# Attention and feed-forward on one core: normalisation in pieces, a gating product moved behind a low part, and running clocks for VectorE's work

## The chip, the cores and the metric

One core of one Trainium2 chip runs the whole kernel. The metric is the device time in microseconds (us) of one execution; the time before is the median of 3 runs.

## What is computed

x has 2048 rows of 512. Two branches are mixed by a gate per row:

```python
g = sigmoid((x * gate_w).sum(-1, keepdims=True))
# A: 32 query heads of 16 on one key/value head
q = (x @ wq) in 32 heads;  k = x @ wk;  v = x @ wv
p = softmax(q @ k.T * 16 ** -0.5);  a = (p @ v, heads joined) @ wo
# B: feed-forward, 512 -> 1792 -> 512
b = silu(x @ w1) @ w2
out = g * a + (1 - g) * b
```

All inputs and the output are float32.

## The kernel before, in words

TensorE's array is used in tiles of 64 rows by 32 columns: eight matmuls of 512 columns run side by side, and such a group of eight is called a **slot** here. Float32 accuracy is had by splitting operands into two 16-bit parts (three products of parts for one).

`attention` (line 726) emits, in an order written out by hand, 32 **rounds** (4 chunks of 512 query rows, 4 groups of 8 heads, 2 halves of a group) of 16 **key steps**. One key step is two score groups: `scores` (L1022) makes one slot of S (L1032), and ScalarE takes its exponential into P (L1035). The product of P with v (`pv`, L1061, matmuls L1078) has two forms. A **split** step uses P's upper 16 bits and a **low part** L that VectorE makes by a subtraction (`low`, L1045 to L1056, two per step): two slots. A **native** step multiplies P in float32: four slots. Only even steps can be split; odd ones are native. `split_step` (L1041) decides: not the first step of a round, and VectorE's backlog below 1.0.

Two key steps make one **cycle** (the loop at L1102). The strings `SPLIT`, `NATIVE` and `PAIR` give its slots: S a score group, F a slot of other matrix work, P one of the two products of a split step, N a native step, B a place for the bound (below). A split cycle is `SFFFSFFFSPPSBN`: 16 slots. **Pair stretches** are three cycles in a row with 8 F each; the second and third end the two F-products of the feed-forward's first layer.

The F slots come from `stream` (L923). It runs the outputs in a fixed order, two at a time: one on the array's upper 64 rows, the next on its lower ones, each into one of two PSUM banks (`pM`). When an output has ended, its eviction is emitted, and the next F slot needs the bank that it frees. Evictions are:

- `ffn_h` (L806): ScalarE's Tanh (L814), then VectorE's **gating product** (L815) in the same breath, then two GpSimd operations (L818, L819) that write H.
- `ffn_o` and `out_proj`: one VectorE accumulation (`add_out`, L736, L745 or L747).
- `q_block` (L840): two VectorE operations (L850, L851), a magnitude (L863) and a DMA.

`bound` (L871) makes a small product for the scores' shift and evicts it on VectorE (L879).

At a round's end `pv` calls `norm_a` (L969): two transposes of the PSUM banks pv (L973, L974), their sum (L975), the digits (L977 to L980), a reciprocal and the quotient into C (L982, L985), all at once. The next round's first product needs the two banks. After a group's second half, `norm_b` (a transpose, L989) and `norm_c` (two operations, L124, L125) follow by `put`, a list of VectorE work with a latest cycle.

`fill` (L782), called at a cycle's end, takes work from that list, then one weight piece (L199, L200) or one operand range check (L139 and L649 to L672), when there is room. Room is reckoned for a cycle at a time: a length of 3.7 or 4.1, less what `spend` (L775) noted, less the backlog that was left.

The emitted order is each engine's order. VectorE, ScalarE, TensorE, GpSimd and the DMA queues wait for each other by semaphores alone.

Of the kernel before, what the change touches and what calls it, by code (L numbers as in the profile page):

```python
# [21 lines left out]
NF = max(GF)  # L22
# [9 lines left out]
        {SPLIT: "SFFFFSFFFFSPPSBN", NATIVE: "SFFFFSFFFFSNBSN"})  # L32

# [16 lines left out]
def kernel(  # L50
# [675 lines left out]
    def attention(ctx, scale_of, t_scale, shifts, split_pieces, chores, q_todo, bounds, early, gates_):  # L726
# [29 lines left out]
        class Out:  # L756


            def __init__(self, terms, evict, hidden=False, is_q=False):
                self.hidden, self.is_q = hidden, is_q  # L760
                self.mm = [(l, r, i, j) for l, r in terms for i, j in ((0, 0), (0, 1), (1, 0))]
                self.evict = evict
# [10 lines left out]
        backlog, spent, todo, cycle = [0.0], [0.0], [], [0]  # L773

        def spend(t):  # L775
            spent[0] += t
# [5 lines left out]
        def fill(length):  # L782
            room = length - backlog[0] - spent[0]
            cycle[0] += 1
            backlog[0], spent[0] = max(0.0, -room), 0.0
            if bounds and turn[0] and turn[1] == 6 and not turn[0].hidden and not turn[0].is_q:
                return
            while todo and (todo[0][0] <= room or cycle[0] >= todo[0][1]):
                t, _, f = todo.pop(0)
                f()  # L790
                room -= t
            if split_pieces.left() and (room >= 1.3 or split_pieces.count < 5.6 + 0.57 * cycle[0]):
                split_pieces.step()
                room -= 1.3
            elif not split_pieces.left() and chores and (room >= 1.1 or cycle[0] > 200):
                if chores[0]:
                    chores[0].pop(0)()
                    room -= 1.1
                elif not open_q:
                    chores.pop(1)()  # L800
                    room -= 1.1
                    if len(chores) == 1:
                        chores.clear()
            backlog[0] = max(0.0, -room)

        def ffn_h(k, f):  # L806
# [4 lines left out]
            def evict(ph):  # L811
# [3 lines left out]
                nc.vector.scalar_tensor_tensor(e, e, 1.0, ph, op0=OP.add, op1=OP.mult)  # L815
# [6 lines left out]
            return Out([(lambda i, b, m, n=32, kt=kt: w1s[b, i, kt, f0 + m:f0 + m + n],  # L822
                         lambda j, b, kt=kt: xs[b, j, kt, cs]) for kt in range(KD)], evict, hidden=1 + f % 2)
# [16 lines left out]
        def q_block(n):  # L840
# [4 lines left out]
            def evict(pq):  # L845
# [5 lines left out]
                nc.vector.scalar_tensor_tensor(q2[:, 1], pq, qsc, q2[:, 0], op0=OP.mult, op1=OP.subtract)  # L851
                nc.sync.dma_start(qd[o, c], q2)
# [7 lines left out]
                spend(1.45)  # L860

            def magnitude(qa):
# [6 lines left out]
                         lambda j, b, kt=kt: xs[b, j, kt, c * 512:c * 512 + 512]) for kt in range(KD)], evict, is_q=True)  # L869

        def bound():  # L871
# [3 lines left out]
            ahead.append(next(seq))  # L875
            ahead[0].bank = pM.tile([128, 512], F32, name="pm")
# [4 lines left out]
            spend(0.6)  # L881
            put(0.6, 3, lambda: (note(), open_q.pop()))
# [26 lines left out]
        def follow():  # L909
# [3 lines left out]
            if o is not None:  # L913
                o.bank = pM.tile([128, 512], F32, name="pm")
            return o

# [6 lines left out]
        def stream():  # L923

            cur = None
            while True:
                if plain[0] and cur is None:
# [7 lines left out]
                    o.evict(o.bank)  # L935
                    yield True
# [7 lines left out]
                if cur and drains[0] == cur.count and ending[0]:  # L944
                    drain()
                for i in range(n):
                    turn[:] = cur, n - i - 1
# [7 lines left out]
                if cur:  # L955
                    cur.evict(cur.bank)
# [225 lines left out]
```

## Time and profile before

| what | value |
|---|---|
| median of 3 runs | 1094.44 us |
| lowest and highest | 1094.07 and 1095.62 us |
| the profiled execution, its time | 1097.11 us |
| its span, first to last instruction | 1095.2 us |
| mean granted TensorE clock | 0.993 |
| instructions in the trace | 63374 |

The profile names engines PE (TensorE matmul), PEld (its weight load), DVE (VectorE), ACT (ScalarE), POOL (GpSimd) and SP (DMA queue). A row of groups has line, engine, operation, output and inputs with their shapes and count, then busy us and mean ns of one, then the idle time ahead of them and what ended it. A row of the timeline has start us, length us and the same names; a number in brackets is the idle time ahead of it and its releaser. The page's table in 40 slices shows PE busy at 9 tenths or more in all slices but the first and the last, ACT from the third to the 39th, DVE between 7 and 9 tenths from the second to the 39th.

### The profile page before, as it was taken

Reading aid. Unit: us, or ns where it says so; the run is one execution under the profiler, and the core shown is the slowest. Engines: PE = TensorE matmul, PEld = TensorE weight load, DVE = VectorE, ACT = ScalarE, POOL = GpSimd, SP = SyncE. Lnnn points to the kernel's source line nnn. Section 1 sums busy time; section 2 is a strip of 40 time slices with the busy share of each in tenths; the row PEclk is TensorE's granted clock in tenths of the full one; section 3 lists DMA queues with packets and bytes.
Section 4 is the critical chain, followed back from the end, with each engine's and each line's share of the span. In section 5 each row is a group of like instructions: output and inputs, shape, how many; then the busy total and the mean of one; then the engine's idle time right before and its main releaser. Section 6 shows DMA issues by size and latency. Waiting matters only on the chain.

```text
span 1095.2 us, 63374 instructions
## 1 busy us (share of the span) xinstructions
PE 1050.2 (96%) x29790; PEld 577.0 (53%) x29790; DVE 899.7 (82%) x1206; ACT 1012.1 (92%) x1121; POOL 215.0 (20%) x170
## 2 busy tenths in 40 slices
PE   8999999999999999999999999999999999999996
PEld 5355556555555445444555555565554555555452
DVE  5779878789988898988879887878789788777975
ACT  5699999999999999999999999999999999999991
POOL 1145205030310220502022004031102014050200
PEclk9899999999999999999999999999999999999999
DMA  5311111210001000000000010000000010000001
GB/s 204 112 49 33 53 53 35 60 50 25 9 21 40 21 21 12 4 21 11 21 12 19 25 39 12 21 12 11 15 13 9 11 50 12 11 12 11 4 4 42
DMA packets 20832, 32.80 MB, mean 30 GB/s; under 512 B 5137, under 2 KB 12050, under 8 KB 20562
## 3 DMA queue, kind: packets, MB, share of 16 engines
q1 hardware_dynamic: 17618, 20.46, 5.9%
q0 software_dynamic: 2512, 8.13, 2.7%
q8 instruction: 235, 3.85, 1.5%
q14 instruction: 35, 0.29, 0.1%
q10 hardware_dynamic: 432, 0.07, 0.0%
HBM read 20.12 MB, written 8.52 MB: 26 GB/s over the span
## 4 chain that ended last, share of the span: by engine, by line
PE 66%; DVE 26%; ACT 5%; issue 2%; DMA 0%; another core or an unknown queue 0%; ACTq 0%; POOL 0%; DVEq 0%
PE pv L1078 23%; PE pm L766 23%; PE S L1032 16%; DVE L L1056 10%; ACT P L1035 4%; DVE T L975 1%; DVE T L973 1%; DVE U L974 1%; DVE e L815 1%; ACT e L814 1%; PE pm L770 1%; DVE O L124 1%; DVE mxs L139 1%; DVE C L985 1%; DVE acc L747 1%
## 5 line engine op out<-in xcount | busy, mean ns | idle before, releaser
L1035 ACT ACTIVATE P<-S 128x1024 f32<-128x1024 f32 x1024 | 968.4, 1067 | 44.0 <-PE S L1032 32.8
L1056 DVE TENSOR_TENSOR L<-P 128x1024 f16<-128x1024 f32 x430 | 531.0, 1281 | 11.1 <-ACT P L1035 11.1
L1032 PE MATMUL S<-qb,KT 50*32 50x512 f16 x8192 | 476.1, 380 | 2.5 <-ACT P L1035 1.4
L1078 PE MATMUL pv<-P,VF 64*32 64x512 f32 x4752 | 333.1, 593 | 0.0
L1032 PEld LDWEIGHTS <-KT 50*32 50x32 f16 x8192 | 189.9, 90 | 229.5 <-issue 158.7
L766 PE MATMUL pm<-w2s,H 64*32 64x512 f16 x5184 | 256.3, 376 | 7.3 <-DVE qx L851 3.1
L766 PE MATMUL pm<-xs,w1s 64*32 64x512 f16 x5376 | 237.7, 376 | 4.1 <-DVE e L815 2.6
L818 POOL CAST H<-e 128x512 f16<-128x512 f32 x56 | 85.2, 1521 | 641.3 <-DVE e L815 639.9
L766 PEld LDWEIGHTS <-w1s 64*32 64x32 f16 x5376 | 119.2, 93 | 64.3 <-issue 20.9
L766 PEld LDWEIGHTS <-H 64*32 64x32 f16 x5184 | 120.4, 93 | 60.4 <-issue 18.8
L1078 PEld LDWEIGHTS pv<-P,VF 64*32 64x32 f32 x4752 | 103.0, 107 | 29.4 <-issue 4.0
L1078 PE MATMUL pv<-L,VP 64*32 64x512 f16 x1720 | 113.6, 375 | 4.5 <-DVE L L1056 3.4
L819 POOL TENSOR_TENSOR H<-e,H 128x512 f16<-128x512 f32 x56 | 106.5, 1902 | 4.5
L1078 PEld LDWEIGHTS <-VP 64*32 64x32 f16 x3440 | 71.0, 93 | 54.0 <-issue 29.4
L1078 PE MATMUL pv<-P,VP 64*32 64x512 bf16 x1720 | 99.4, 388 | 0.0
L766 PE MATMUL pm<-xs,wqs 64*32 64x512 f16 x1152 | 82.8, 375 | 4.2 <-DVE e L815 2.6
L815 DVE SCALAR_TENSOR_TENSOR e<-e,pm 128x512 f32<-128x512 f32 x56 | 38.1, 681 | 40.0 <-ACT e L814 39.8
L973 DVE STREAM_TRANSPOSE T<-pv 128x512 f32<-128x512 f32 x32 | 22.9, 717 | 55.5 <-PE pv L1078 52.9
L766 PE MATMUL pm<-wo_s,O 64*32 64x512 f16 x1440 | 64.3, 375 | 1.1 <-DVE e L815 0.7
L747 DVE SCALAR_TENSOR_TENSOR acc<-pm,g,acc 128x512 f32<-128x512 f32 x48 | 35.8, 746 | 26.5 <-PE pm L766 23.9
L766 PEld LDWEIGHTS <-wqs 64*32 64x32 f16 x1152 | 37.3, 92 | 18.2 <-issue 4.8
L182 POOL DMA_DIRECT2D raw<-in_B_w_dram x27 | 15.3, 568 | 141.8 <-DVE w1s L200 72.3
(168 smaller groups left out, 506.7 us busy)
## 6 DMA issues: line engine op xcount, KB each, us to landing
qb<-qd SPq DMA_DIRECT2D x192, 32.0 KB
raw<-in_B_w_dram POOLq DMA_DIRECT2D x23, 256.0 KB, 3.0
xn<-in_A_x_dram SPq DMA_DIRECT2D x8, 512.0 KB
out_dram<-acc SPq DMA_DIRECT2D x16, 256.0 KB
qd<-qx SPq DMA_DIRECT2D x12, 256.0 KB
raw<-in_A_wo_dram POOLq DMA_DIRECT2D x4, 256.0 KB, 3.0
qb<-sh SPq DMA_DIRECT2D x62, 2.0 KB
raw<-in_B_w_dram SPq DMA_DIRECT2D x3, 256.0 KB
```

The source lines that it names most:

```text
L124: nc.vector.tensor_copy(a1, a)
L182: queue.dma_start(r, src)
L747: nc.vector.scalar_tensor_tensor(a, po, gate[:, n:n + 1], a, op0=OP.mult, op1=OP.add)
L766: nc.tensor.matmul(self.bank[32 * m:32 * m + 32], l(i, rows, 32 * m), r(j, rows), start=first, stop=last)
L815: nc.vector.scalar_tensor_tensor(e, e, 1.0, ph, op0=OP.add, op1=OP.mult)
L818: nc.gpsimd.tensor_copy(H[:, 0], e)
L819: nc.gpsimd.tensor_tensor(H[:, 1], e, H[:, 0], op=OP.subtract)
L973: nc.vector.transpose(T, pv[0])
L1032: nc.tensor.matmul(sc[32 * m:32 * m + 32, f], KT[b:b + 50, k0:k0 + 32], qtile[i][b:b + 50, j], start=True, stop=True)
L1035: nc.scalar.activation(P[:, 2 * j:2 * j + 2], sc, AF.Exp, scale=scale_of(c, o))
L1056: nc.vector.tensor_tensor(lows[s][:, q], P[:, q], upper(P)[:, q], op=OP.subtract)
L1078: nc.tensor.matmul(pvs[i][h][32 * j:32 * j + 32], a[r], b[r, j], start=first, stop=last)
```

## The change

Four things are edited, all inside `attention`; the arithmetic is the same.

- **Normalisation in pieces.** `norm_a` emits only the two transposes. The sum, the digits and the quotient become three entries of the `put` list, due 2, 2 and 3 cycles on. The digits use a small buffer z of their own instead of U. `norm_b` is due 4 cycles on, `norm_c` 2 after it.
- **Gating product.** `ffn_h`'s eviction emits the Tanh and appends the rest to a list `waiting`. `gates_now` empties it behind the next low part that `scores` emits, and at the latest ahead of the next bank or the cycle's end.
- **Running clocks.** `spend`, room and backlog go. `pe`, `act` and `dve` hold estimated times: `on_pe` and `on_dve` advance them per emitted piece of work, with costs written in. Work from the list is emitted when DVE's clock stays within `ROOM` = 2.1 of PE's, or when it is due.
- **Native steps.** `split_step` asks whether DVE's clock is less than `SLACK` = 1.2 past the end of the step's exponentials; a round's first step may be split too.

```diff
+SLACK, ROOM = 1.2, 2.1
...
+        pe, act, dve = [0.0], [0.0], [0.0]
+        def on_dve(t, after=0.0):
+            dve[0] = max(dve[0], after) + t
+            return dve[0]
+        def on_pe(t, after=0.0):
+            pe[0] = max(pe[0], after) + t
...
         def add_out(c, t, po, gate):
             n = c * 4 + t
-            spend(0.68)
...
+            return on_dve(0.74, pe[0])
...
-        def fill(length):
-            room = length - backlog[0] - spent[0]
+        def fits(t):
+            return max(dve[0], pe[0]) + t <= pe[0] + ROOM
+        def fill():
             cycle[0] += 1
...
-            while todo and (todo[0][0] <= room or cycle[0] >= todo[0][1]):
+            while todo and (fits(todo[0][0]) or cycle[0] >= todo[0][1]):
                 t, _, f = todo.pop(0)
+                on_dve(t, pe[0])
                 f()
-                room -= t
-            if split_pieces.left() and (room >= 1.3 or split_pieces.count < 5.6 + 0.57 * cycle[0]):
+            if split_pieces.left() and (fits(1.1) or split_pieces.count < 5.6 + 0.57 * cycle[0]):
+                on_dve(1.1, pe[0])
                 split_pieces.step()
...
                 nc.scalar.activation(e, ph, AF.Tanh, scale=t_scale)
-                nc.vector.scalar_tensor_tensor(e, e, 1.0, ph, op0=OP.add, op1=OP.mult)
-                H = Hs[k, f] = wp.tile([128, 2, 512], F16, name="H", bufs=2 * NF)
-                spend(0.69)
-                nc.gpsimd.tensor_copy(H[:, 0], e)
-                nc.gpsimd.tensor_tensor(H[:, 1], e, H[:, 0], op=OP.subtract)
+                act[0] = max(act[0], pe[0]) + 0.5
+                ready = act[0] + 0.1
+                def gate():
+                    nc.vector.scalar_tensor_tensor(e, e, 1.0, ph, op0=OP.add, op1=OP.mult)
+                    H = Hs[k, f] = wp.tile([128, 2, 512], F16, name="H", bufs=2 * NF)
+                    nc.gpsimd.tensor_copy(H[:, 0], e)
+                    nc.gpsimd.tensor_tensor(H[:, 1], e, H[:, 0], op=OP.subtract)
+                    freed[0] = on_dve(0.68, ready)
+                waiting.append(gate)
+                return 1e9
...
         def follow():
...
             if o is not None:
+                gates_now()
                 o.bank = pM.tile([128, 512], F32, name="pm")
+                o.free = freed[0]
             return o
+        def gates_now():
+            while waiting:
+                waiting.pop(0)()
...
         def norm_a(pv, rb, st):
...
             nc.vector.transpose(T, pv[0])
             nc.vector.transpose(U, pv[1])
-            nc.vector.tensor_tensor(T, T, U, op=OP.add)
-            z = U3[:, :, 0:DIGITS]
...
+            on_dve(1.38, pe[0])
+            def turned():
+                nc.vector.tensor_tensor(T, T, U, op=OP.add)
+            def joined():
+                z = wp.tile([128, 16, 1 + DIGITS], F32, name="z")
...
+            def quotient():
+                r = wp.tile([128, 16, 1], F32, name="rr")
+                nc.vector.reciprocal(r, T3[:, :, 16:17])
...
+            put(0.7, 2, turned)
+            put(1.1, 2, joined)
+            put(0.68, 3, quotient)
...
             if lq and lq[0][0] <= p - 2 and not bound_now():
                 low(*lq.pop(0))
+                gates_now()
         def split_step(s):
-            return steps[s][1] > 0 and backlog[0] < 1.0
+            return dve[0] - ends[2 * s] < SLACK
...
                 norm_a(pvs.pop(i), rb, state)
-                spend(3.1)
                 if rb == 1:
-                    put(0.65, 3, lambda: (norm_b(state), put(1.0, 3, lambda: norm_c(state, (c, o)))))
+                    put(0.7, 4, lambda: (norm_b(state), put(1.1, 2, lambda: norm_c(state, (c, o)))))
...
-            fill(4.1 if pair[0] or ended[0] and ended[0].hidden else 3.7)
+            gates_now()
+            fill()
```

More of the change, by code (lines that the diff above doesn't have):

```diff
@@ L880, in bound @@
             note = q_shift(o, c, s1)
-            spend(0.6)
-            put(0.6, 3, lambda: (note(), open_q.pop()))
+            on_pe(0.06)
+            ahead[0].free = on_dve(0.68, pe[0])
+            put(0.67, 3, lambda: (note(), open_q.pop()))
         urgent = []
@@ L945, in stream @@
                     drain()
+                if new:
+                    pe[0] = max(pe[0], new.free)
                 for i in range(n):
+                    on_pe(0.2165)
                     turn[:] = cur, n - i - 1
@@ L1011, in prefetch @@
                     load_q(qtile[i], c, o, rb, shifts)
-        probs, lows, lq, native = {}, {}, [], set()
+        probs, lows, lq, native, ends, low_end = {}, {}, [], set(), {}, {}
         bounded = [False]
         def bound_now():
-            return bounds and ended[0] and not bounded[0] and not ended[0].hidden and not ended[0].is_q
+            return bounds and ended[0] and not bounded[0] and ended[0].kind == "o"
         def scores(p):
@@ L1075, in pv @@
                     probs.pop(s)
+            on_pe(0.866 if n == 3 else 0.2165, ends[2 * s + 1])
             for j in range(4):
@@ L1115, in attention @@
                 slots = FIRST
-            if not pair[0] and debt[0] >= 6 and s and turn[0] and turn[0].hidden == 1 and turn[1] == 12:
+            if not pair[0] and debt[0] >= 6 and s and turn[0] and turn[0].pair and turn[1] == 12:
                 pair[0] = 3
```

62 lines of the change are left out of this document (33 added, 29 removed).

## The prediction

> **What bounds the kernel now.** I read the page from the top: busy shares, the chain that ended last, the costliest groups.
>
> ```profile
> PE 1050.2 (96%) x29790; PEld 577.0 (53%) x29790; DVE 899.7 (82%) x1206; ACT 1012.1 (92%) x1121; POOL 215.0 (20%) x170
> PE 66%; DVE 26%; ACT 5%; issue 2%; DMA 0%; another core or an unknown queue 0%; ACTq 0%; POOL 0%; DVEq 0%
> L1035 ACT ACTIVATE P<-S 128x1024 f32<-128x1024 f32 x1024 | 968.4, 1067 | 44.0 <-PE S L1032 32.8
> L815 DVE SCALAR_TENSOR_TENSOR e<-e,pm 128x512 f32<-128x512 f32 x56 | 38.1, 681 | 40.0 <-ACT e L814 39.8
> ```
>
> TensorE and ScalarE are both nearly full, yet VectorE, busy 82%, holds 26% of the chain: at places it is late and the other two wait. Shares do not say where, so I cut the loop into its cycles of two key steps (four score groups S each) at the starts of S in the timeline, and asked the busy time of each stretch. The columns are length; PE, PEld, DVE, ACT, POOL busy; granted clock; DMA.
>
> ```profile
> 46.25:1067.01 1020.76, 992.38 (x29293) 547.77 (x29300) 850.63 (x1086) 980.87 (x1072) 208.60 (x142) 1.00 0.09 24
> 421.79:425.46 3.67, 3.67 (x120) 2.00 (x112) 3.02 (x4) 3.67 (x5) 0.00 (x0) 1.00 0.00 0
> 1044.85:1048.74 3.89, 3.89 (x120) 2.08 (x112) 3.46 (x10) 3.89 (x5) 0.00 (x0) 1.00 0.02 4
> 1048.74:1052.34 3.60, 3.27 (x96) 1.58 (x88) 3.60 (x5) 3.54 (x5) 0.00 (x0) 1.00 0.00 0
> 553.79:557.70 3.91, 3.91 (x136) 2.17 (x128) 3.60 (x4) 3.80 (x5) 0.00 (x0) 1.00 0.01 4
> 557.70:561.89 4.19, 4.10 (x137) 2.10 (x128) 2.12 (x4) 4.19 (x6) 1.26 (x1) 1.00 0.00 0
> 561.89:565.93 4.04, 4.04 (x136) 2.10 (x121) 2.29 (x3) 4.04 (x6) 2.48 (x3) 1.00 0.04 10
> 823.71:828.04 4.33, 4.33 (x143) 2.13 (x134) 3.92 (x10) 4.21 (x5) 0.00 (x0) 1.00 0.08 19
> 503.90:510.09 6.19, 4.91 (x137) 2.28 (x128) 5.72 (x12) 5.10 (x6) 0.85 (x1) 1.00 0.03 8
> 404.83:410.73 5.90, 4.29 (x128) 2.17 (x114) 4.92 (x12) 3.85 (x5) 0.00 (x0) 1.00 0.08 20
> 118.83:124.57 5.74, 4.05 (x124) 1.92 (x116) 5.71 (x9) 4.02 (x5) 0.55 (x1) 1.00 0.30 96
> 790.21:798.13 7.92, 6.82 (x122) 2.55 (x127) 5.55 (x11) 4.53 (x5) 1.52 (x2) 0.78 0.11 29
> 46.25:52.94 6.69, 6.69 (x87) 2.89 (x93) 4.74 (x11) 3.51 (x4) 1.57 (x3) 0.51 0.66 186
> ```
>
> The first row is the loop from its second cycle to its last. The next seven are cycles without a stall: split 3.67; native (two exact products) 3.89; split right behind a native one 3.60; the three cycles of a pair stretch 3.91, 4.19, 4.04 (the last two with a Tanh and its gating product); a native one among those 4.33, which over its 20 slots of PE is 0.2165 a slot. The order as built has, in those 254 cycles, 143 split, 28 native, 2 plain ones with a Tanh (4.04), 22, 21 and 25 of the three pair places, and 13 native pair cycles: 524.8 + 108.9 + 8.1 + 86.0 + 88.0 + 101.0 + 56.3 = 973.1 us. The loop took 1020.8, so **47.7 us are lost to stalls**; the last five rows are five of them. The row at 503.90 in detail, DVE first, then ACT and PE:
>
> ```profile
> 504.20 0.72 DVE L973 STREAM_TRANSPOSE T<-pv 128x512 f32<-128x512 f32 x1 [2.85 <-PE pv L1078]
> 505.55 0.69 DVE L975 TENSOR_TENSOR T<-T,U 128x512 f32<-128x512 f32 x1
> 506.27 0.26 DVE L977 TENSOR_TENSOR U<-T,mu 128x96 f32<-128x96 f32 x1
> 507.15 0.25 DVE L982 RECIPROCAL rr<-T 128x16 f32<-128x16 f32 x1
> 507.89 0.71 DVE L989 STREAM_TRANSPOSE T<-C 128x512 f32<-128x512 f32 x1
> 508.53 0.65 DVE L815 SCALAR_TENSOR_TENSOR e<-e,pm 128x512 f32<-128x512 f32 x1
> 505.43 0.62 ACT L814 ACTIVATE e<-pm 128x512 f32<-128x512 f32 x1
> 509.23 0.37 PE L766 MATMUL pm<-xs,wqs 64*32 64x512 f16 x1 [1.28 <-DVE e L815]
> ```
>
> At a round's end (32 of them) the normalisation stands on DVE in one block: two transposes 1.35 us (504.20 to 505.55), their sum 0.72, the digits 0.88, the quotient 0.74, here the transpose back 0.64. The Tanh was done at 506.05; its gating product, which frees PE's bank, began at 508.53, and PE went on at 509.23. Cycles 404.83 and 118.83 are alike, with other evictions behind the block.
>
> **The change, part by part.**
>
> *Split and native.* The built order of the changed kernel has 117 split cycles, 54 native, 2 with a Tanh, 17, 25 and 26 pair ones and 13 native pair ones: 429.4 + 210.1 + 8.1 + 66.5 + 104.8 + 105.0 + 56.3 = 980.1. That is **+7.0 us**; 20 more split cycles stand right behind a native one, at 3.60, which takes back 1.4: **+5.6**. A native step also drops two low parts (378 in the order for 430), here two of them and what follows:
>
> ```profile
> 427.12 2.36 DVE L1056 TENSOR_TENSOR L<-P 128x1024 f16<-128x1024 f32 x2 [0.31 <-ACT P L1035]
> 429.40 1.21 DVE L139 TENSOR_REDUCE mxs<-w2s 128x1 f32<-128x1024 f16 x1
> 424.46 2.35 DVE L1056 TENSOR_TENSOR L<-P 128x1024 f16<-128x1024 f32 x2
> 423.75 0.42 PE L1078 MATMUL pv<-P,VP 64*32 64x512 bf16 x8
> ```
>
> One holds DVE 1.14 us (427.12 to 429.40), so 59 us of DVE work go, but off the path: they show only where DVE is late, which the stalls below count.
>
> *Normalisation in pieces.* Work is the same; only the transposes stay at the round's end. In the order, sum and digits still leave together 22 times, so the largest block behind the transposes is 1.6 us instead of 2.3 to 3.0.
>
> *Gating product behind the next low part* (55 of 56). A typical pair cycle shows the room:
>
> ```profile
> 557.42 1.93 ACT L1035 ACTIVATE P<-S 128x1024 f32<-128x1024 f32 x2
> 559.88 0.69 DVE L815 SCALAR_TENSOR_TENSOR e<-e,pm 128x512 f32<-128x512 f32 x1 [2.07 <-ACT e L814]
> 560.48 1.22 DVE L1056 TENSOR_TENSOR L<-P 128x1024 f16<-128x1024 f32 x1
> 561.02 0.41 PE L766 MATMUL pm<-xs,w1s 64*32 64x512 f16 x8
> ```
>
> DVE waits 2.07 us for the Tanh while the low part could run: its exponential was done at 559.35. In the new order: low part from 559.4 to 560.5, product to 561.2, where PE wants the bank at 561.02. So it is 0.2 late in the middle pair cycle, and in the last one, where two exponentials stand ahead of the Tanh, not at all. Behind the product on DVE stand the second low part, used a cycle later, and the pieces; GpSimd's casts start later by at most 1.1 us, and it is busy 20%. No queue but DVE's is passed.
>
> *What stays lost.* (a) In 12 middle pair cycles transposes or pieces stand right ahead of low part and product. For the row at 503.90: transposes from 0.30 after the cycle's start, 1.35, sum 0.72, low part 1.14, product 0.65: 4.16, where PE wants the bank at 3.32 (561.02 - 557.70). 0.84 late; where only transposes or one piece lead, about 0.3, behind two pieces up to 1.2. I take 0.7: 8.4 us. Such lateness shows nearly whole: 6.19 was 1.86 over the native 4.33, with the product 1.96 late. (b) The other 15 middle ones, 0.2 each: 3.0. (c) Round ends now carry low parts ahead of the transposes. With an accumulation in the cycle, the low parts from 424.46 end 1.27 after the next cycle begins, the transposes at 2.62, while the next round's first product wants its bank at 1.96 (423.75 - 421.79). 0.66 late in 9 rounds, of which ScalarE's pace covers about half: 2.7. (d) Scattered small ones elsewhere: 2.0, an estimate between nothing and 20 times the 0.29 by which 4.19 exceeds its 18 slots.
>
> *Start.* Step 0 is now split, so two low parts (2.27) stand ahead of the bound's eviction:
>
> ```profile
> 44.86 0.39 PE L367 MATMUL pm<-qx,kab 64*32 64x512 f16 x2 [2.06 <-DVE O L851]
> 45.66 0.68 DVE L879 TENSOR_SCALAR qx<-pm 64x512 f16<-64x512 f32 x1
> ```
>
> That eviction ends at 48.6 instead of 46.3, and PE's next product waits for it. The cycle at 46.25 runs at a granted clock of 0.51 and takes 6.69, 2.8 over a native one. The new one has 15 slots to go at 48.6: 10 at half clock until 52.9, 5 at full clock, end at 54.0, 1.0 later than now; if the half clock lasts through it, 2.2 later. I take 1.0: start 3.8. The Trainium skill, "TensorE: Matmul & The Clock Gate", section "HAM oscillation — how this bites in real kernels", says that PE should have no idle gap above about 3.4 us. The trace differs: a gap of 2.06 us stands right before the half clock; by the page a longer start wait would cost no clock, and the start would stay at 1.0.
>
> *Range check* (a DMA to DRAM and back).
>
> ```profile
> SPq L658 <- DMA md<-raw: 7.9, 1, 7.9
> ```
>
> In the cycle at 790.21 this write was still to land; it is 4.0 over a native one, by a stall and a clock of 0.78. I keep it. The check now follows the gather by two cycles instead of three, so DVE may wait up to 2 us for the row: +1.0, bounds 0 and 2.2 (below nothing if the pause falls elsewhere: -4.0).
>
> *Sum.* Lost after: 3.8 + 5.0 + 8.4 + 3.0 + 2.7 + 2.0 = 24.9 against 47.7, so -22.8; cycles +5.6: **-17.2 us**. Renamed buffer z, planner constants and the tail behind the loop cost nothing: same instructions, and the last normalisation is one chain as now. Span 1095.2 becomes 1078.0; the profiled execution, 1097.1, 1079.9; it stood 2.7 over the median of 1094.44, so **1077 us**.
>
> **Rivals.**
> 1. *ScalarE covers the rest.* (a) to (d) vanish because PE, with 3.46 us of slots in a 3.67 cycle, catches up: 16 us less, 1061. For: short waits are made good in the split cycles. Against: 6.19 showed no cover.
> 2. *DVE is still late at round ends.* Two low parts and the transposes meet where the old order had a free DVE (2.85 us idle ahead of 504.20, the round's first step being native). If (a) to (d) cost 27 instead of 16: 1088. If they cost 33, nothing is gained.
> 3. *Slower: the product becomes PE's wait.* Behind a whole low part (1.14, less the 0.46 between 560.56 and 561.02) in both pair cycles, 54 times 0.68 is 36.7, where (a) and (b) hold 11.4: 1102. It decides from 0.53 us a product on. For: PE's banks are two and it waits for one at 509.23. Against: DVE's 2.07 idle ahead of the product.
> 4. *The pieces are none.* In the order sum and digits leave together 22 times, and the sum leaves with the transposes 10 times. If such blocks hold up what PE waits for as the whole one does, 17 of the 24.8 us taken as recovered at round ends (40.9 now, 16.1 after) stay lost and pay for the native cycles: 1094, no change. Against: the block in front of a product shrinks from 3.0 or more to 1.6.
>
> **How the numbers follow.** Forecast, 1077 give or take 7: 0.52. Rival 1: 0.15. Rival 2: 0.18. Rival 4: 0.05. Rival 3: 0.10. The range from 1061 to 1092 takes in rivals 1 and 2 and leaves out 3 and most of 4. About 0.2%, 2 us, is what a measurement of this kernel can tell from no change: faster 0.85, same 0.05, slower 0.10.
>
> **What would show it.** Right: the cycles after a round's end fall from 6.2 to about 5, no DVE block over 1.6 us between transposes and product; DVE's idle time ahead of the product (39.8) falls by half or more; low parts x378; native cycles still 3.89. Wrong: PE waiting for e in ordinary middle pair cycles by 0.5 or more (rival 3), PE waiting for U at the first product of most rounds (rival 2), or half clock in more windows than now. What would upset the sum is a price per native cycle other than 0.22.

## The result and the profile after

The changed kernel took 1085.29 us (median of 4 runs, 1085.09 to 1085.50) beside 1095.03 for the kernel before: ratio 0.991, 95% interval 0.9892 to 0.9927. The profiled execution took 1085.09 (1097.11 before): 12.0 less where 17.2 were forecast. The 1085.29 stands between the forecast (1077 give or take 7) and rival 2's 1088.

The page of the changed kernel, the lines that answer to those shown of before (busy shares, the chain that ended last, three of the costliest groups):

```profile
PE 1047.3 (97%) x29790; PEld 577.1 (53%) x29790; DVE 846.5 (78%) x1154; ACT 1012.0 (93%) x1121; POOL 178.2 (16%) x170
PE 69%; DVE 19%; ACT 9%; issue 2%; POOL 0%; DMA 0%; ACTq 0%; SPq 0%; POOLq 0%; DVEq 0%
L1080 ACT ACTIVATE P<-S 128x1024 f32<-128x1024 f32 x1024 | 968.3, 1062 | 31.0 <-PE S L1077 20.0
L1104 DVE TENSOR_TENSOR L<-P 128x1024 f16<-128x1024 f32 x378 | 470.5, 1274 | 101.7 <-ACT P L1080 101.3
L829 DVE SCALAR_TENSOR_TENSOR e<-e,pm 128x512 f32<-128x512 f32 x56 | 38.1, 680 | 1.6 <-ACT e L824 0.6
```

DVE's share of the chain fell from 26% to 19%. The exponential waited 31.0 us, 13.0 less than before: about the whole gain. DVE's 40.0 idle us ahead of the gating product are 1.6 now; it waits 101.7 ahead of low parts instead (11.1 before). By itself that is free time on DVE and not yet a shorter program; e5 below tries it alone. Low parts are 378, as forecast.

Windows of the changed kernel: the loop, a split and a native cycle, and the cycles that answer to the stalled ones of before (length; PE, PEld, DVE, ACT, POOL busy; clock; DMA):

```profile
46.32:1054.94 1008.62, 989.38 (x29305) 547.58 (x29312) 798.26 (x1035) 980.89 (x1072) 171.82 (x142) 1.00 0.09 24
807.51:811.18 3.67, 3.67 (x121) 1.99 (x112) 3.36 (x4) 3.67 (x5) 0.00 (x0) 1.00 0.02 4
121.02:124.91 3.89, 3.89 (x120) 2.19 (x112) 3.82 (x8) 3.84 (x5) 0.00 (x0) 1.00 0.20 72
403.13:406.83 3.70, 3.70 (x122) 2.00 (x114) 2.66 (x5) 3.64 (x5) 0.00 (x0) 1.00 0.08 23
498.45:503.44 4.99, 4.46 (x137) 2.06 (x129) 4.66 (x6) 4.69 (x6) 0.85 (x1) 1.00 0.02 4
783.17:788.90 5.73, 3.88 (x115) 1.98 (x119) 5.70 (x9) 4.15 (x5) 2.70 (x2) 1.00 0.04 10
46.32:54.29 7.97, 5.87 (x87) 2.89 (x93) 6.71 (x12) 3.58 (x4) 1.67 (x3) 0.57 0.51 155
244.08:249.02 4.94, 3.86 (x120) 2.14 (x112) 4.94 (x7) 3.87 (x5) 0.00 (x0) 1.00 0.04 11
382.13:387.69 5.56, 4.28 (x136) 2.00 (x128) 5.49 (x7) 4.89 (x6) 0.84 (x1) 1.00 0.01 3
```

The loop is 1008.62 for 1020.76, so the whole change lies in it. Split and native cycles still cost 3.67 and 3.89. Two cycles behind a round's end that took 5.90 and 5.74 (404.83, 118.83) now take 3.70 and 3.89, the one of 6.19 takes 4.99. At the prediction's prices the order costs 980.1 us and **28.5 are lost** (47.7 before; 47.6 in the table below, where only the total is rounded): 4.3 in the second cycle of all, 14.1 in middle pair cycles, 3.0 at the range check (the cycle at 783.17 and the one ahead of it), 7.1 elsewhere. The last two rows are kinds of stall that need a reason: a round's end at 244.08 and a middle pair cycle at 382.13.

The first of them on DVE in the changed kernel, and the two products of PE that waited (a number in brackets is the idle time ahead):

```profile
243.41 0.74 DVE L757 SCALAR_TENSOR_TENSOR acc<-pm,g,acc 128x512 f32<-128x512 f32 x1
244.07 2.35 DVE L1104 TENSOR_TENSOR L<-P 128x1024 f16<-128x1024 f32 x2
246.33 0.71 DVE L1006 STREAM_TRANSPOSE T<-pv 128x512 f32<-128x512 f32 x1
246.97 0.67 DVE L1007 STREAM_TRANSPOSE U<-pv 128x512 f32<-128x512 f32 x1
...
247.09 0.38 PE L1129 MATMUL pv<-P,VP 64*32 64x512 bf16 x1 [0.86 <-DVE T L1006]
247.69 0.42 PE L1129 MATMUL pv<-P,VP 64*32 64x512 bf16 x7 [0.21 <-DVE U L1007]
```

Two low parts of the new round's first step, now split, stand ahead of the transposes. PE wants the bank that they empty and waits 0.86 and then 0.21. How often this happens, beside the largest of PE's waits in the loop (us in all, times, the longest):

```profile
PE pm L779 <- DVE e L829: 9.9, 13, 1.6
PE pv L1129 <- DVE U L1007: 1.5, 7, 0.2
PE pv L1129 <- DVE T L1006: 0.9, 1, 0.9
```

So the picture at 244.08 is the only one of its size; with the smaller ones the transposes hold PE for 2.4 us in all, and the gating product for 9.9.

### The profile page after: what moved, and what is told of

The parts are those of the page before. It is cut to its first block, busy times and chain, and to the rows that moved or that the text cites. A ratio compares the mean times of both kernels' runs of the same rounds, so it can differ in the third digit from the quotient of the medians.

```text
span 1083.2 us, 63321 instructions
## 1 busy us (share of the span) xinstructions
PE 1047.3 (97%) x29790; PEld 577.1 (53%) x29790; DVE 846.5 (78%) x1154; ACT 1012.0 (93%) x1121; POOL 178.2 (16%) x170
## 4 chain that ended last, share of the span: by engine, by line
PE 69%; DVE 19%; ACT 9%; issue 2%; POOL 0%; DMA 0%; ACTq 0%; SPq 0%; POOLq 0%; DVEq 0%
PE pm L779 25%; PE pv L1129 24%; PE S L1077 17%; DVE L L1104 9%; ACT P L1080 8%; DVE e L829 2%; DVE T L1006 1%; DVE U L1007 1%; PE pt L318 1%; PE pm L783 1%; ACT e L824 1%; DVE T L1011 1%; DVE z L1015 0%; DVE acc L757 0%; PE pk L132 0%
## 5 line engine op out<-in xcount | busy, mean ns | idle before, releaser
L1104 DVE TENSOR_TENSOR L<-P 128x1024 f16<-128x1024 f32 x378 | 470.5, 1274 | 101.7 <-ACT P L1080 101.3
L1077 PE MATMUL S<-qb,KT 50*32 50x512 f16 x8192 | 457.0, 380 | 3.6 <-ACT P L1080 1.2
L1129 PE MATMUL pv<-P,VF 64*32 64x512 f32 x5168 | 352.5, 590 | 0.0
L779 PE MATMUL pm<-w2s,H 64*32 64x512 f16 x5184 | 251.6, 375 | 4.7 <-DVE e L829 4.2
L779 PEld LDWEIGHTS <-w1s 64*32 64x32 f16 x5376 | 112.2, 93 | 70.9 <-issue 27.1
L1129 PE MATMUL pv<-P,VP 64*32 64x512 bf16 x1512 | 90.7, 390 | 2.3 <-DVE U L1007 1.5
L1129 PE MATMUL pv<-L,VP 64*32 64x512 f16 x1512 | 86.3, 375 | 0.1
L832 POOL TENSOR_TENSOR H<-e,H 128x512 f16<-128x512 f32 x56 | 71.5, 1276 | 4.5
L1129 PEld LDWEIGHTS <-VP 64*32 64x32 f16 x3024 | 56.1, 94 | 29.2 <-issue 9.8
L757 DVE SCALAR_TENSOR_TENSOR acc<-pm,g,acc 128x512 f32<-128x512 f32 x48 | 35.8, 745 | 40.8 <-PE pm L779 38.6
L779 PEld LDWEIGHTS <-O 64*32 64x32 f16 x1440 | 31.0, 93 | 15.7 <-issue 3.9
L184 POOL DMA_DIRECT2D raw<-in_B_w_dram x27 | 14.8, 550 | 120.9 <-DVE w1s L202 69.9
```

The costliest lines, as they stand in the source:

```text
L184: queue.dma_start(r, src)
L757: nc.vector.scalar_tensor_tensor(a, po, gate[:, n:n + 1], a, op0=OP.mult, op1=OP.add)
L779: nc.tensor.matmul(self.bank[32 * m:32 * m + 32], l(i, rows, 32 * m), r(j, rows), start=first, stop=last)
L1077: nc.tensor.matmul(sc[32 * m:32 * m + 32, f], KT[b:b + 50, k0:k0 + 32], qtile[i][b:b + 50, j], start=True, stop=True)
L1104: nc.vector.tensor_tensor(lows[s][:, q], P[:, q], upper(P)[:, q], op=OP.subtract)
L1129: nc.tensor.matmul(pvs[i][h][32 * j:32 * j + 32], a[r], b[r, j], start=first, stop=last)
```

## The experiments

All ratios are those of medians, to the kernel before on the same chip. The runs were on several chips, on which the kernel before had medians of 1093.42 to 1095.31. For each trace the cycles were also cut at the starts of S and priced as in the prediction. "Lost" is the loop less the price; "ends" are the first three cycles of the rounds without middle pair ones.

| kernel | median us | ratio, 95% interval | native | price | lost | of it 2nd cycle | middle pair | ends |
|---|---|---|---|---|---|---|---|---|
| before | 1095.03 | 1 | 41 | 973.1 | 47.6 | 2.8 | 13.8 | 19.8 |
| changed | 1085.29 | 0.991 (0.9892-0.9927) | 67 | 980.1 | 28.5 | 4.3 | 14.1 | 6.8 |
| e1 pieces only | 1069.54 | 0.9772 (0.9755-0.9788) | 45 | 974.3 | 18.3 | -0.2 | 3.1 | 4.6 |
| e2 product at once | 1089.54 | 0.9949 (0.9934-0.9965) | 67 | 980.1 | 31.0 | 3.3 | 5.9 | 14.6 |
| e3 whole block | 1120.28 | 1.0254 (1.0228-1.0279) | 67 | 980.1 | 62.6 | 3.0 | 26.6 | 29.4 |
| e4 slack 2.4 | 1083.50 | 0.9896 (0.9878-0.9914) | 22 | 968.8 | 38.6 | 4.3 | 12.7 | 11.2 |
| e5 pieces, queued | 1071.45 | 0.9782 (0.9769-0.9795) | 45 | 974.3 | 20.5 | 2.6 | 7.5 | 3.8 |
| e6 mixed | 1085.92 | 0.9916 (0.9903-0.993) | 67 | 980.1 | 28.6 | 3.8 | 2.4 | 10.5 |
| e7 step 0 native | 1081.20 | 0.9881 (0.9864-0.9899) | 68 | 980.2 | 23.3 | -0.2 | 14.2 | 5.9 |
| e8 e1, no rule | 1081.82 | 0.9879 (0.9862-0.9896) | 35 | 971.8 | 32.1 | 0.1 | 6.1 | 13.9 |
| e9 rule back | 1080.86 | 0.9887 (0.9861-0.9912) | 87 | 985.1 | 17.6 | -0.2 | 14.8 | 0.2 |
| e10 rule, slack 2.4 | 1069.54 | 0.9774 (0.9748-0.9799) | 41 | 973.3 | 19.3 | -0.2 | 10.6 | 0.7 |
| e11 e1, rule alone | 1081.71 | 0.9881 (0.9856-0.9906) | 32 | 971.6 | 32.0 | 0.1 | 6.0 | 4.7 |
| e12 e10, no piece | 1073.78 | 0.9804 (0.9784-0.9824) | 46 | 974.8 | 21.8 | 2.7 | 4.6 | 1.9 |

Theory 1 at the outset: the pieces are the gain; product behind a low part, native cycles and start give some of it back. Its rivals put the gain into the moved product (A) or the clocks (B).

**e1, the pieces alone** in the kernel before:

```diff
-            nc.vector.tensor_tensor(T, T, U, op=OP.add)
...
+            put(0.7, 2, turned)
+            put(1.1, 2, joined)
+            put(0.68, 3, quotient)
...
-                spend(3.1)
+                spend(1.38)
...
-                    put(0.65, 3, lambda: (norm_b(state), put(1.0, 3, lambda: norm_c(state, (c, o)))))
+                    put(0.7, 4, lambda: (norm_b(state), put(1.1, 2, lambda: norm_c(state, (c, o)))))
```

> The kernel before, with one part of the change: behind a round's two transposes the sum, the digits and the quotient leave as three pieces in later cycles. The old planner (a length of 3.7 or 4.1 less what was charged), the old rule for native steps and the product at once behind the Tanh stay; the order has 422 low parts (430 before, 378 after) and 45 native cycles (41, 67). Theory 1 (the gain is the normalisation broken up; the late product and the native cycles give some of it back): at least the whole change's gain, because the product stays early and there are only 4 native cycles more (0.9 us): 1078 to 1086. Rival A (the gain comes from the product moved off DVE's 39.8 us of waiting): 1091 to 1096, as before. Rival B (it comes from the running clocks, which place native steps where DVE is late): 1089 to 1095.

1069.54: 25 faster than before and 16 faster than the whole change, 8 beyond theory 1's range. The pieces are more than the whole gain; A and B fall as sources of it. What gives 16 us back?

Two things stand in the way of reading the 25 as the smaller block alone. In 20 of the 31 rounds that end in the loop the list had room at once, so sum and digits still left right behind the transposes and only the quotient went to a later cycle. And from the loop's cycle 66 on (counted from 0) the pair stretches stand in other cycles than before: the output projections enter the F slots after `norm_c`, which here leaves at cycle 68 and in the kernel before at cycle 66. Five middle pair cycles (81, 97, 113, 129 and 241) then no longer follow a round's end, where they lost 9.4 us together. The changed kernel, e2, e3, e6, e7 and e9 have the old places but for one stretch; e4, e5, e10, e11 and e12 have those of e1, e10 up to cycle 195. e3 and e8 tell the pieces and the places apart.

**e2, the product at once** in the changed kernel, the order else kept:

```diff
                 def gate():
-                    nc.vector.scalar_tensor_tensor(e, e, 1.0, ph, op0=OP.add, op1=OP.mult)
-                    H = Hs[k, f] = wp.tile([128, 2, 512], F16, name="H", bufs=2 * NF)
-                    nc.gpsimd.tensor_copy(H[:, 0], e)
-                    nc.gpsimd.tensor_tensor(H[:, 1], e, H[:, 0], op=OP.subtract)
                     freed[0] = on_dve(0.68, ready)
```

The four lines stand ahead of `def gate` here.

> The changed kernel, but the gating product and GpSimd's two operations stand right behind the Tanh as before, the clocks being kept as they were so that all else in the order is the same (378 low parts, 67 native cycles). Theory 1 (behind the low part the product frees the bank late in the middle pair cycles, 13.7 us in all over the 4.19 of one without a stall): most of that comes back, 1074 to 1080. Rival A (the gain comes from the moved product): 1090 to 1096. Rival C (the low part that now waits behind the product, and the Tanh, is as late for its second product as the product was for the bank): 1083 to 1087, as after.

1089.54, missed by all three: 4 slower than the changed kernel. The middle pair cycles did gain (14.1 to 5.9), but the round ends lost as much (6.8 to 14.6): PE's waits for the transposes rose from 2.4 us to 7.8. Only 2.5 of the 5.1 us between the two profiled executions lie in the loop; 1.8 lie ahead of it, where e2's clock is at 0.50 from 45.5 us on, and 0.9 behind it.

**e3, the whole block** in the changed kernel:

```diff
-            put(0.7, 2, turned)
-            put(1.1, 2, joined)
-            put(0.68, 3, quotient)
+            turned()
+            joined()
+            quotient()
+            put(0.7, 2, lambda: None)
+            put(1.1, 2, lambda: None)
+            put(0.68, 3, lambda: None)
```

> The changed kernel, but sum, digits and quotient leave in one block behind the two transposes, as in the kernel before; three empty pieces hold their places in the planner so that all else in the order is the same (378 low parts, 67 native cycles). Theory 1 (the pieces are the whole gain, and what else changed costs): slower than the kernel before, 1096 to 1108, since the block now stands with low parts and the late product. Rival A or B (product or clocks are the gain, and the pieces matter little): 1085 to 1089. The prediction's fourth rival (the pieces are none): 1084 to 1087.

1120.28, slower still than theory 1 said. The rest of the order is the same here, the places of the pair stretches too, so in the changed order the pieces alone are worth 35 us (34 of them in the loop). In the old one it was 25: whatever else the change does makes DVE later where the block stands.

**e4, slack 2.4**:

```diff
-SLACK, ROOM = 1.2, 2.1
+SLACK, ROOM = 2.4, 2.1
```

> The changed kernel with one number changed: a step is split as long as the running clock of DVE stands less than 2.4 us, not 1.2, behind the step's exponential. The order has 468 low parts (378 after) and 22 native cycles (67), so DVE gets 103 us more work. Theory 1 (many native steps relieve a DVE that isn't late): 45 native cycles fewer at up to 0.22 are 10 us, of which some goes in new waits: 1076 to 1084. Rival B (native steps where DVE is late are the gain): DVE is late at the rounds' ends again, 1089 to 1100.

1083.50, within theory 1's range, yet hardly a gain: 45 native cycles fewer save 11.3 of price and lose 10.1 in new waits. So native cycles do relieve something, only not all of them at a profit.

**e5, e1 with the product queued** behind the next low part:

```diff
+                def gate():
                     nc.vector.scalar_tensor_tensor(e, e, 1.0, ph, op0=OP.add, op1=OP.mult)
...
+                waiting.append(gate)
...
                 low(*lq.pop(0))
+                gates_now()
```

> The kernel of e1 (1069.5; pieces, old planner, 422 low parts, 45 native cycles) with the gating product and GpSimd's two operations queued behind the next low part, as in the change; every other instruction stays in its place, so that this is the queueing alone. Theory 1 (the queued product frees the bank late in the middle pair cycles, which lost 14.0 in the changed kernel and 3.1 in e1): 8 to 12 slower than e1, 1077 to 1082, with middle pair cycles of 4.33 to 4.5 where e1 has about 4.3. Rival D (the queueing is free, and the 16 us between e1 and the changed kernel belong to the clocks, which choose other cycles for pieces and native steps): 1068 to 1072.

1071.45: rival D. The intervals of e1 and e5 overlap. The middle pair cycles lose 4.4 more and the split ones 4.6 less; 2.8 of the rest are a half clock in the second cycle that e1 doesn't have. **Theory 1's late product falls.**

**e6, the product at once in the middle pair cycle only**, the changed kernel else:

```diff
+                now = pair[0] == 2
+                if now:
+                    product()
...
                 def gate():
+                    if not now:
+                        product()
                     freed[0] = on_dve(0.68, ready)
```

`product` holds the four lines of the product.

> The changed kernel, but the product stands right behind its Tanh in the middle pair cycle alone and behind the low part elsewhere; clocks and order otherwise as in the changed kernel. e2, with all products early, lost only 6.0 in the middle pair cycles but 10 more in split, native and first pair cycles. Theory 1: the last cycle of a stretch, where the queued product cost nothing (0.9 over 26 cycles), keeps its free place, so the middle ones gain without the rest losing all of it: 1077 to 1083. Rival C (the clocks have put pieces where DVE is free only if it doesn't wait for the Tanh, so the early product makes the cycles behind it late whichever it is): 1084 to 1090.

1085.92: rival C. The middle pair cycles lost 2.4 for 14.1, and other cycles 11.8 more. The wait went elsewhere: 9.7 of these 11.8 lie two cycles behind a middle pair one, 0.3 in the cycle right behind it. The work on DVE is the same in sum, but why it shows there no run separates.

**e7, step 0 native** in the changed kernel:

```diff
-            return dve[0] - ends[2 * s] < SLACK
+            return s > 0 and dve[0] - ends[2 * s] < SLACK
```

> The changed kernel with step 0 native again (376 low parts, 68 native cycles), so that no low parts stand ahead of the bound's first eviction. Theory 1 (the start's second cycle, 7.97 now and 3.73 in e1, is long by a wait behind those low parts and by a half clock that follows): 1.3 to 4.3 faster than the changed kernel, 1081 to 1084. Rival (only the phase of the clock's fall matters, since e1 has the same gap of 2.06 ahead of it and no half clock): 1085 or, if the fall happens to stay away, 1082.

1081.20, 4.1 less and at theory 1's end. The profiled execution has neither the wait nor the half clock, so this run doesn't tell the two apart. Elsewhere a half clock without that wait cost 2.6 to 2.8 in the second cycle (before, e5, e12), which would leave some 1.5 of the changed kernel's 4.3 to the wait, an estimate.

**e8, e1 without the rule that a round's first step is native**:

```diff
-            return steps[s][1] > 0 and backlog[0] < 1.0
+            return s > 0 and backlog[0] < 1.0
```

> The kernel of e1 without the rule that a round's first step is native (except step 0), so native steps come only from the old planner's backlog: 442 low parts, 35 native cycles for 45; by class prices 972.1 for 974.6. Theory 1 (in pieces, a round's end needs no relief by a native step): 1066 to 1069. Rival E (the native first step is what leaves DVE free for the transposes, and two low parts ahead of them make PE wait at the next round's first product): 0.5 to 1 in most of 31 rounds, 1074 to 1090.

1081.82: rival E, 12 slower for 10 native cycles less; 30 of the rounds' 32 first steps turned split and 20 others native. This rule went with the change, beside the clocks. The same cycle of step 306 in e8 (one of 5.05 us) and, second, in e1 (3.90):

```profile
653.26 2.76 DVE L1066 TENSOR_TENSOR L<-P 128x1024 f16<-128x1024 f32 x2
655.95 0.70 DVE L973 STREAM_TRANSPOSE T<-pv 128x512 f32<-128x512 f32 x1
656.58 0.67 DVE L974 STREAM_TRANSPOSE U<-pv 128x512 f32<-128x512 f32 x1
...
656.70 0.38 PE L1088 MATMUL pv<-P,VP 64*32 64x512 bf16 x1 [0.88 <-DVE T L973]
657.30 0.42 PE L1088 MATMUL pv<-P,VP 64*32 64x512 bf16 x7 [0.21 <-DVE U L974]
```

```profile
644.87 0.72 DVE L973 STREAM_TRANSPOSE T<-pv 128x512 f32<-128x512 f32 x1 [1.69 <-PE pv L1088]
645.51 0.67 DVE L974 STREAM_TRANSPOSE U<-pv 128x512 f32<-128x512 f32 x1
646.22 0.69 DVE L977 TENSOR_TENSOR T<-T,U 128x512 f32<-128x512 f32 x1
```

In e8 the two low parts hold the transposes to 2.4 us after the cycle's start (653.58), in e1 nothing does: they follow PE's last product at once, 0.3 us after the cycle's start (644.57). It is the picture of the changed kernel at 244.08, and more often: in e8 PE waits 7.4 us for the transposes, in e1 not at all.

e8 also settles what e1 left open. Up to cycle 129 its pair stretches stand where those of the kernel before do, and the middle cycles 81, 97 and 113, which lost 1.86 each behind a round's end, lose nothing. Cycle 97 before, then in e8:

```profile
436.72:442.91 6.19, 4.91 (x139) 2.28 (x130) 5.74 (x12) 5.08 (x6) 0.87 (x1) 1.00 0.03 8
```

```profile
430.31:434.50 4.19, 4.19 (x136) 2.40 (x128) 3.43 (x6) 4.19 (x6) 1.26 (x1) 1.00 0.04 11
```

So the pieces do it without new places. In cycles 2 to 65, where the places are those of before in all kernels, e1 lost 3.6 less than the kernel before and e8 3.3 more than e1.

**Theory 2**: the loss of 14 against e5 belongs to the new native rule, which takes native steps away from the rounds' first ones (3 of 32 are left) and puts them where they relieve less. Rival F: the clocks place the pieces badly, whatever the rule.

**e9, the rule back** in the changed kernel; **e10, the same with slack 2.4**:

```diff
-            return dve[0] - ends[2 * s] < SLACK
+            return steps[s][1] > 0 and dve[0] - ends[2 * s] < SLACK
```

> The changed kernel with the old rule added to its new one: a round's first step is native always, other steps by the running clocks as before. 338 low parts, 87 native cycles (67 in the changed kernel, of which 3 stand first in a round); by class prices 985.4 for 980.4. Theory 2 (theory 1's late product fell with e5; the 16 us lost against e1 belong to the new native rule, which leaves a round's first step split, as taking the rule from e1 cost 12 in e8): the stalls fall by 12 or more, the class prices rise by 5, so 1073 to 1080. Rival F (the clocks put pieces into the wrong cycles, whatever the rule): 1084 to 1092.

> The kernel of e9 with the slack of the clocks at 2.4 us instead of 1.2: 430 low parts, 41 native cycles, 32 of them a round's first; by class prices 973.5. Theory 2: the natives that count are kept and those that relieve nothing are gone, so about e5's 1071.5 with 1.1 less in class prices: 1066 to 1072. Rival F: like e4 (1083.5), which has the same slack without the rule: 1080 to 1085. If all natives beside the first ones were relief, it would be slower than e9.

1080.86, a touch over the range in which theory 2 had it and below F's, and 1069.54, right in it. The stall at 244.08 is gone, here in e10, the cycle and its DVE rows:

```profile
236.88:240.78 3.90, 3.90 (x121) 2.14 (x113) 3.65 (x6) 3.90 (x5) 0.00 (x0) 1.00 0.05 11
```

```profile
236.23 0.74 DVE L757 SCALAR_TENSOR_TENSOR acc<-pm,g,acc 128x512 f32<-128x512 f32 x1
237.18 0.72 DVE L1006 STREAM_TRANSPOSE T<-pv 128x512 f32<-128x512 f32 x1 [0.21 <-PE pv L1129]
237.82 0.67 DVE L1007 STREAM_TRANSPOSE U<-pv 128x512 f32<-128x512 f32 x1
```

The cycle is 0.23 dearer by price and 1.04 shorter. The four kernels make a table of two by two: without the rule 1085.29 and 1083.50 (slack 1.2, 2.4), with it 1080.86 and 1069.54. At slack 2.4 the rule adds 19 native cycles (4.5 us by price) and takes 19.3 of losses; at slack 1.2 it adds 20 (5.0) and takes 10.9; 4.5 of either are the second cycle. Given the rule, the 46 native cycles that slack 1.2 adds over 2.4 cost 11.8 and take 1.7: they relieve next to nothing. The slack also moves the list's pieces and, from cycle 66 on, the pair stretches, so this is the slack's whole effect. In cycles 2 to 65, with the places alike, nine more native cycles cost 2.1 and the losses rise by 0.4, so the reading doesn't hang on the places.

**e11, e1 with the rule alone** and no native step by backlog:

```diff
-            return steps[s][1] > 0 and backlog[0] < 1.0
+            return steps[s][1] > 0 and backlog[0] < 90.0
```

> The kernel of e1 with native steps at the rounds' first steps alone (the backlog may grow without limit): 448 low parts, 32 native cycles for 45; by class prices 971.8 for 974.6. Theory 2 (only a native step at a round's end is worth its 0.22): 2 to 3 faster than e1, 1066 to 1068. Rival G (the other 13 stand where DVE is late and spare a wait each): 1070 to 1078.

1081.71: nearest rival G, though 3.7 beyond its range, so theory 2 was too strong. The rule isn't enough: 13 native cycles by backlog, 2.7 us of price, spare 13.7, together with the list, whose order follows the same backlog. 9.8 of these lie ahead of the loop's cycle 60, where weights are still split on DVE (16.6 lost there, 6.8 in e1).

Theory 2 is also too strong on where the 14 us go. Of the 13.8 us by which the changed kernel's loop is longer than e5's, 5.8 are the price of 22 more native cycles, 6.6 lie in the middle pair cycles, 3.0 at the round ends and 1.7 in the second cycle; the rest is 3.3 shorter. PE waits 9.9 us for the gating product in the changed kernel and 2.7 in e5, which queues it too. With clocks and queue the middle pair cycles lose 10.6 to 14.8 (changed, e4, e9, e10), with the old planner and the queue 7.5. So what the clocks put ahead of the product has a part in it, and no run separates that part from the places of the stretches.

**e12, e10 with nothing of the planner's list ahead of a middle pair cycle**:

```diff
+            if pair[0] == 3:
+                return
             while todo and (fits(todo[0][0]) or cycle[0] >= todo[0][1]):
```

> The kernel of e10 (1069.5) in which nothing of the planner's list (pieces of the normalisation, splits, range check) leaves at the end of the first cycle of a pair stretch, so that on DVE low part and gating product of the middle cycle have nothing of it ahead; 420 low parts, 46 native cycles, by class prices 975.0 for 973.5. In e10 a piece left there in 23 of 27 stretches, and the middle cycles lost 10.6. Theory 3 (what the middle cycles still lose is the work ahead of the low part, and the queued product itself costs at most 0.23 there): 4 to 5 off the middle cycles, 1.5 on for the native ones: 1065 to 1068. Rival H (work kept from one cycle is late in the next, as in e6): 1069 to 1074.

1073.78: rival H. The middle pair cycles fell from 10.6 to 4.6 (0.17 each), more than theory 3 said. Against these 6.0 stand 1.5 of price, 2.9 of a half clock in the second cycle, and 5.6 in the other cycles. As in e6, much of the wait moved: up to cycle 204, where the stretches of e10 and e12 stand alike, the middle cycles lose 4.0 less, and those two and four cycles behind them 3.4 more. No run beat e1 and e10, 2.3% faster than before and 1.4% faster than the change.

## Why the prediction was right, and where it was not

The sign and the stated range (1061 to 1092) held, the size did not: 1085.29 lies above the forecast's own 1070 to 1084. At the profiled execution 1079.9 was forecast and 1085.09 came, 5.2 more. The forecast had also taken 2.7 off for the median; the changed kernel's profiled execution stands at its median.

- *Split and native.* The prices held (3.67, 3.89, and 3.60 behind a native cycle). What the prediction left out is what a native cycle spares at its place: it priced 26 more of them at +5.6, left the relief to the stalls, and put no figure on the 29 rounds that lose theirs in the first step. Where they stand decides. Without the second cycle, 31 more first-step cycles and 13 fewer others take 14.8 us of stalls for 4.3 of price at slack 2.4 (e4, e10); 28 more and 9 fewer take 6.4 for 4.8 at slack 1.2 (changed, e9); 30 fewer and 20 more, in e8, bring 13.5 and save 2.5. That is about 0.5, 0.2 and 0.5 us a first step, an estimate that gives the others nothing, and they cost 0.22 to 0.25. One of the others that slack 1.2 adds takes 0.04 for 0.26 (1.7 and 11.8 over 46).
- *Round ends.* Rival 2 named the mechanism, two low parts and the transposes meeting; its 1088 was 3 too high. Of that wait itself, (c), the prediction had the size nearly right: 2.7 in 9 rounds, and PE waits 2.4 in 8. So it isn't what made the forecast too low; it is part of what the old rule would have saved.
- *Normalisation in pieces.* Right. The prediction had 24.8 us recovered outside the start and the range check (40.9 to 16.1); 19.7 came (40.9 to 21.2). Alone in the old order the pieces, with the places that move with them, are worth 25.3 (from 1094.84, the kernel before in e1's comparison). Rival 4 falls by e3, where the whole block costs 35. That sum and digits left together 24 times in e1 cost little there. Rival 1 falls too: the losses (a) to (d) that it lets vanish came to 21.2.
- *Gating product.* DVE's wait went, as said. As a price the queueing is nothing, by e5; in the changed kernel PE waits 9.9 us for the product, but e6 and e12 took much of such a wait away without a gain. Rival 3 falls.
- *(a) and (b)* gave the sizes nearly right: 11.4 forecast, 14.1 measured. By what DVE had ahead of the low part: two steps of the list, or the transposes and one, in 11 cycles, 8.4 us; one or none in 16 cycles, 5.6, where 3.0 was forecast. The cycle at 498.45 lost 0.80 over 4.19 where 0.84 was worked out:

```profile
498.75 0.72 DVE L1006 STREAM_TRANSPOSE T<-pv 128x512 f32<-128x512 f32 x1 [0.60 <-PE pv L1129]
499.39 0.68 DVE L1007 STREAM_TRANSPOSE U<-pv 128x512 f32<-128x512 f32 x1
500.10 0.69 DVE L1011 TENSOR_TENSOR T<-T,U 128x512 f32<-128x512 f32 x1
500.71 1.22 DVE L1104 TENSOR_TENSOR L<-P 128x1024 f16<-128x1024 f32 x1
501.84 0.68 DVE L829 SCALAR_TENSOR_TENSOR e<-e,pm 128x512 f32<-128x512 f32 x1
```

One of the three dearest, at 382.13, had more ahead than any row of before suggested, on DVE, then PE and GpSimd:

```profile
380.03 3.20 DVE L1104 TENSOR_TENSOR L<-P 128x1024 f16<-128x1024 f32 x2
383.16 0.70 DVE L1033 STREAM_TRANSPOSE T<-C 128x512 f32<-128x512 f32 x1
383.89 0.43 DVE L126 CAST O<-T 128x512 f16<-128x512 f32 x1
384.36 0.69 DVE L127 TENSOR_TENSOR O<-T,O 128x512 f16<-128x512 f32 x1
384.96 1.22 DVE L1104 TENSOR_TENSOR L<-P 128x1024 f16<-128x1024 f32 x1
386.10 0.68 DVE L829 SCALAR_TENSOR_TENSOR e<-e,pm 128x512 f32<-128x512 f32 x1
...
386.83 0.37 PE L779 MATMUL pm<-xs,wqs 64*32 64x512 f16 x1 [1.19 <-DVE e L829]
...
379.79 1.22 POOL L832 TENSOR_TENSOR H<-e,H 128x512 f16<-128x512 f32 x1
```

Two low parts took 3.20 for 2.35, the first beside GpSimd's subtract (the last section has more on that), and the transpose back and the two operations of the cast, which the prediction didn't list, left together, 1.9 us: PE waited 1.19.

- *(c) and (d)*: 7.1 measured where 4.7 was forecast, less the 1.4 that it credited to cheap cycles: +3.8, the largest term that was mis-sized. With (c) at 2.4, most of it is (d).
- *Start*: 3.8 forecast over a native cycle; 4.1 measured (7.97 less 3.89). *Range check*: 5.0 forecast, 3.0 measured. The check did come too early, as the prediction said: DVE waited 3.57 us for the row (2 at most was forecast) and PE 1.63 for the product behind it; what fell away is the half clock of before.

```profile
782.02 0.39 DVE L666 TENSOR_REDUCE raw<-raw 1x32 f32<-1x128 f32 x1 [3.57 <-DMA raw<-md]
...
785.22 0.84 PE L779 MATMUL pm<-w2s,H 64*32 64x512 f16 x24 [1.63 <-DVE e L829]
```

Together: +0.5 at the start (counted over its own price, 4.3), -2.0, +2.7 in the middle pair cycles, +3.8 elsewhere: 5.0 of the 5.2.

Open: whether another slack or backlog gives less than e1 and e10, and what the range check would cost if it were read later; no run tried them.

## What to carry to other kernels

Price a relief by what stands behind it at its place: here a native step first in a round bought some 0.2 to 0.5 us for about 0.24, and others almost nothing or 1 us (e10, e11). When an order is rewritten, look for the rule that went out with the old planner, and change one part at a time: one part of this change was worth 2.3%, the others took 1.4 of that back. See too what else an edit moves: e1 also moved the pair stretches, and only e3 and e8 told the two apart. A wait that was removed by reordering an engine's queue, without taking work off it, stood a few cycles further on here (e6, e12).

## What the runs showed of the hardware

The same wait of PE ahead of the loop is followed by a half clock in some executions and not in others. The changed kernel, then e7: PE's gap, and the next cycle's window (the granted clock is the number ahead of the DMA share):

```profile
45.03 0.39 PE L369 MATMUL pm<-qx,kab 64*32 64x512 f16 x2 [2.06 <-DVE O L868]
48.82 0.62 PE L779 MATMUL pm<-xs,w1s 64*32 64x512 f16 x4 [2.10 <-DVE qx L899]
```

```profile
44.83 0.39 PE L369 MATMUL pm<-qx,kab 64*32 64x512 f16 x2 [2.05 <-DVE O L868]
```

```profile
46.10:49.80 3.70, 3.70 (x89) 2.18 (x96) 3.10 (x7) 3.20 (x4) 0.99 (x2) 1.00 0.55 172
```

In all 14 profiled executions this gap is 2.05 to 2.07 us. Behind it the clock stays at 1.00 in e1, e7, e9 and e10, and falls to 0.50 in the other ten: for 3.4 us from 45.5 in e8, for 6.8 from 47.4 in the changed kernel (which has the second gap too, as e4 and e6 have), for 10.2 from 45.5 in e2. In the second cycle that is 0.51, 0.53 and 0.52 in the kernel before, e5 and e12, which have the one gap alone. The Trainium skill, "TensorE: Matmul & The Clock Gate", section "HAM oscillation — how this bites in real kernels", gives as its rule no idle gap of TensorE above about 3.4 us; e1, e7, e9 and e10 agree, the other ten don't. A gap of 2 us is a risk of some 3 us here (2.8, 2.6 and 2.7 in the second cycles of the kernel before, e5 and e12), not a price; what decides, no run shows. Executions of the kernel before spread as well, on one chip from 1091.60 us at a mean clock of 0.998 to 1098.52 at 0.993.

GpSimd's subtract slows a low part that runs beside it. In the changed kernel's trace 282 low parts run beside neither of GpSimd's two operations on H and take 1.22 us on average, 52 beside its cast 1.22, and 44 beside its subtract 1.70, up to 2.21. The two at 380.03 are such a case: 0.85 more than the 2.35 of an undisturbed pair.
